# Two decode attention blocks on one core: the last projection of B transposed in its operands, and the first weight load cut in two

## The chip, the core and the metric

The kernel runs on one NeuronCore of a Trainium2 chip. The metric is the device time of one execution in microseconds (us), lower is better. Five engines work side by side, each with its own instruction queue: TensorE (PE; its weight loads are listed as PEld), VectorE (DVE), ScalarE (ACT), GpSimd (POOL) and SyncE (SP). Engines wait for each other through semaphores. Transfers between the chip's memory (HBM) and the core's on-chip memory (SBUF, 128 partitions) are issued by an engine, here SP and ACT, and carried out by 16 DMA engines. TensorE writes to PSUM, from where DVE or ACT copy results.

## What is computed

Two independent attention blocks, A and B, each for one query token with 32 heads of 128 elements, over a cache of 8192 positions. Their outputs, 512 numbers each, are put side by side.

```python
q = (x @ wq).reshape(B, Sq, H, Dh).transpose(0, 2, 1, 3)       # x: 1x1x512, wq: 512x4096
scores = einsum("bhqd,bhkd->bhqk", q, k_cache) * Dh ** -0.5    # k_cache: 1x32x8192x128, bf16
p = softmax(scores, axis=-1)
o = einsum("bhqk,bhkd->bhqd", p, v_cache)
y = o.transpose(0, 2, 1, 3).reshape(B, Sq, H * Dh) @ wo        # wo: 4096x512
out = concatenate([yA, yB], axis=-1)                           # 1x1x1024
```

The caches are 64 MiB each, four of them; each of the four weight matrices has 4 MiB. All of it is read once.

## The kernel before

The 64 heads are worked off in 16 rounds of 4 heads, n = 0 to 15; rounds 0 to 7 belong to A. Each round has an 8 MiB tile of k and one of v, both laid out so that a head's 8192 positions lie in 32 partitions with 256 positions each. There are two buffers for k and one for v.

**Start.** ACT issues the two loads of x (1 KB each, one row each), SP the two loads of wq (128 rows of 32 KB each, into the v buffer, which is still free), then k of rounds 0 and 1. TensorE spreads x over the partitions (`xmm`, L264), ACT copies it out (L268), and TensorE multiplies it with wq, 32 instructions for A and 32 for B (`qmm`, L281); in these a group of 4 heads writes 4 times 32 rows of PSUM, so that the query stands repeated in all partitions of its head. ACT copies the queries to SBUF (L287). The load of v of round 0 waits for the last of these matmuls, since it overwrites wq.

**A round.** DVE multiplies k with the query in place (L311, four pieces), TensorE adds up over the 128 elements with an identity matrix (L468), DVE finishes the sums (L316). The maximum goes over DVE and TensorE (L323, L488, L324, L327, L491), ACT takes exponentials (L339), TensorE adds up their sums (L497) and multiplies with v in 256 instructions (L505, 128 columns of weights and 4 moving columns). DVE divides (L345, L346) into `oD`, the attention output with the element within a head in the partitions and the head in the columns.

**SP's order** sets the order of the transfers: SP issues loads one behind another, and each waits for its buffer. k of round n + 2 waits for the sums of round n, v of round n for the v products of round n - 1. In the last rounds come wo of A, the first half of wo of B (group 0), v of round 15 in two pieces, then the rest of wo of B in five ever smaller groups (`WOB`: heads 16 to 23, 24 to 27, 28 and 29, 30, 31). wo of both blocks lies in the first k buffer.

**End.** The output of the earlier rounds is laid out anew for the groups whose rows were loaded as contiguous pieces (`relayout`, L390 to L396). In round 15 TensorE runs, between its scores and its v products, the projection of A (`mm_a`, L409: for each head one column of o repeated 32 times as weights and 512 columns of wo moving, four heads in turn into four blocks of 32 rows), the projection of B for group 0 (`mm_b`, L422) and the sum over the rows of A (L431). After the v products come groups 1 to 5 of `mm_b`. In `mm_b` a piece of wo (128 x 128) is the weight and one column of o moves past it; the result is a column of 128 outputs, four of them side by side in `yps[1]`, one per quarter of the outputs. Then DVE casts these four columns to `yT` (L441), TensorE transposes them to four rows (L442), DVE casts those into `out_b` (L444), and SP stores `out_b` (4 rows of 256 bytes). SP then waits for both stores.

A line number L208 stands for all DMA issues, since a helper records them; L53 is the wait in the emitter, and L534 the start of the engines' programs.

Of the kernel before, what the change touches and what calls it, by code (L numbers as in the profile page):

```python
# [8 lines left out]
BF16 = mybir.dt.bfloat16  # L9
F32 = mybir.dt.float32  # L10

P = 128
# [11 lines left out]
class _Plan:  # L24
# [6 lines left out]
    def wait(self, eng, mark):  # L31
        if mark is None:
            return
        ctr, val = mark
        if val <= 0 or self.waited.get((eng, ctr.name), 0) >= val:
            return
        self.waited[(eng, ctr.name)] = val
        self.prog[eng].append((None, ctr, val))

    def op(self, eng, fn, ctr=None, needs=(), inc=1):  # L40
        for m in needs:
            self.wait(eng, m)
        self.prog[eng].append((fn, ctr, inc))
        if ctr is None:
            return None
        ctr.n += inc
        return ctr, ctr.n
# [28 lines left out]
def bass_concat_heads__mha_block_cached__gqa_block_cached__decode_kernel(  # L76
# [13 lines left out]
    xs = [A_x, B_x]  # L90
    ks = [A_k_cache, B_k_cache]
    vs = [A_v_cache, B_v_cache]
    wqs = [A_wq, B_wq]
    wos = [A_wo, B_wo]
    NA = 2
    H, Sk, Dh = ks[0].shape[1:]
    D = xs[0].shape[2]
    NOUT = wos[0].shape[1]
# [5 lines left out]
    HP = P // G  # L104
# [3 lines left out]
    N = NA * GA  # L108
# [9 lines left out]
    NQ = NOUT // P  # L118

    with ExitStack() as st:  # L120
# [3 lines left out]
        def sb(name, shape, dt):  # L124
            return ec(nc.sbuf_tensor(name, shape, dt))
# [6 lines left out]
        wq_buf = [vflat[:, a * WQ:(a + 1) * WQ] for a in range(NA)]  # L132
        wq_sb = [b.rearrange("p (c n) -> p c n", c=C) for b in wq_buf]
        wo_buf = [kflat[0][:, a * H * NOUT:(a + 1) * H * NOUT] for a in range(NA)]
        wo_sb = [b.rearrange("p (j n) -> p j n", n=NOUT) for b in wo_buf]
# [6 lines left out]
        xrow = sb("xrow", [1, NA, D], BF16)  # L142
# [4 lines left out]
        ident = sb("ident", [P, P], BF16)  # L147
# [7 lines left out]
        oD = sb("oD", [P, NA, H], BF16)  # L155
        zb = sb("zb", [P, 2, P], BF16)
        o2 = sb("o2", [P, NA, H], BF16)
        mask = {g: sb("mask%d" % g, [P, P // g], BF16) for g in RG}
        jsel = {g: sb("jsel%d" % g, [P, g], BF16) for g in RG}
        yT = sb("yT", [P, NQ], BF16)  # L160
        out_a = sb("out_a", [1, NOUT], BF16)
        out_b = sb("out_b", [NQ, P], BF16)

        def ps(name, shape):
            return ec(nc.psum_tensor(name, shape, F32))
# [4 lines left out]
        bmp = ps("bmp", [P, 512])  # L170
        misc = ps("misc", [P, 512])
        yps = [ps("yps%d" % i, [P, 512]) for i in range(2)]

        pl = _Plan()
        op, wait = pl.op, pl.wait

        def ctr(name):
            return _Ctr(nc, st, name)

        s_x = ctr("s_x")  # L180
        s_w = [ctr("s_w%d" % a) for a in range(NA)]
# [4 lines left out]
        s_out = [ctr("s_out%d" % a) for a in range(NA)]  # L186
        c_pool, c_dve, c_act, c_pe = ctr("c_pool"), ctr("c_dve"), ctr("c_act"), ctr("c_pe")
# [19 lines left out]
        def dma(eng, dst, src, c, needs=()):  # L207
            return op(eng, lambda e: e.dma_start(dst, src), c, needs, inc=16)  # L208


        def const(fn, needs=()):
# [6 lines left out]
            out=ident[:], in_=ones_bf[:], pattern=[[1, P]], compare_op=ALU.is_equal,  # L218
            fill=0.0, base=0, channel_multiplier=-1), [i_onesb])
        i_identf = const(lambda e: e.affine_select(  # L220
            out=ident_f[:], in_=ones_f[:], pattern=[[1, P]], compare_op=ALU.is_equal,
# [2 lines left out]
        i_pool = const(lambda e: e.memset(pt[:], 0.0))  # L224


        x_in = [dma("ACT", xrow[0:1, a, :], xs[a][0], s_x) for a in range(NA)][-1]
        wq_in = [dma("SP", wq_buf[a], wqs[a].rearrange("(p c) n -> p (c n)", p=P), s_w[a])
                 for a in range(NA)]
        k_in, v_in = {}, {}  # L230

        def load_k(n):
# [34 lines left out]
        m = op("PE", xmm, c_pe, [x_in, i_pool])  # L267
# [39 lines left out]
        mul_done, sr_done, p_done, o_done = {}, {}, {}, {}  # L307
# [104 lines left out]
        m = op("PE", mm_a, c_pe, [o2_ready[0, 0], woa_in, y_free[0]])  # L412
        ya_ready = op("DVE", lambda e: e.tensor_copy(ya_sb, yps[0][:]), c_dve, [m, mul_done[N - 1, NB - 1]])

        def mm_b(g):
            h0, n, rows = WOB[g]

            def mm(e):
                r = None
                for j in range(h0, h0 + n):  # L420
                    for i in range(NQ):
                        r = e.matmul(yps[1][:, i:i + 1], wo_sb[1][:, j, i * P:(i + 1) * P],  # L422
                                     (o2 if rows else oD)[:, 1, j:j + 1], start=(j == 0 and i == 0),
                                     stop=(j == H - 1 and i == NQ - 1), skip_group_check=True)
                return r
            return op("PE", mm, c_pe, [o2_ready.get((1, h0)) if rows else o_done[N - 1],
                                       wob_in[g], y_free[1]])

        for g in range(NPRE):
            mm_b(g)  # L430
        m = op("PE", lambda e: e.matmul(mtp[0:1, :], part[:], ya_sb, start=True, stop=True),  # L431
               c_pe, [ya_ready, misc_free[0]])
        m = op("ACT", lambda e: e.copy(out_a[:], mtp[0:1, :]), c_act, [m])
# [4 lines left out]
        plan_o(N - 1)  # L438
        for g in range(NPRE, len(WOB)):
            m = mm_b(g)  # L440
        m = op("DVE", lambda e: e.tensor_copy(yT[:], yps[1][:, 0:NQ]), c_dve, [m])  # L441
        m = op("PE", lambda e: e.matmul(bmp[0:NQ, 0:P], yT[:], ident[:], start=True, stop=True),  # L442
               c_pe, [m, p_done[N - 1]])
        m = op("DVE", lambda e: e.tensor_copy(out_b[:], bmp[0:NQ, 0:P]), c_dve, [m])  # L444
        done_b = dma("SP", out[0][:, NOUT:2 * NOUT].rearrange("o (q n) -> (o q) n", q=NQ), out_b[:],
                     s_out[1], [m])
        wait("SP", done_a)
        wait("SP", done_b)

# [99 lines left out]
```

## Time and profile before

| what | value |
|---|---|
| median of 3 runs (lowest to highest) | 668.1 us (667.97 to 668.66) |
| the profiled execution's own time | 668.09 us |
| its span, first to last instruction | 666.4 us |
| mean granted TensorE clock | 0.71 |
| TensorE busy / its weight loads / VectorE / ScalarE | 61% / 36% / 52% / 9% |
| moved by DMA | 285.33 MB, mean 428 GB/s |

The profile is one execution recorded by the hardware profiler. Its time outside the span (668.09 - 666.4 = 1.7 us) holds no instruction. "PE" rows are matmuls, "PEld" rows weight loads; a row of the timeline gives the start, the length, the engine, the line, the operation with its output and inputs, how many instructions were merged, and in brackets how long the engine was idle before and what released it. SPq and ACTq rows are DMA issues. A row of the windows gives for a stretch the busy time and the number of instructions of each engine, the granted clock, the share of the 16 DMA engines that packets cover (all of a packet's length is put down to the stretch in which it starts, so short stretches can exceed 1) and the rate.

### The profile page before, as it was taken

How to read it: one execution, taken by the hardware profiler on the slowest of the kernel's cores; microseconds unless marked ns; L12 is line 12 of the kernel's file. 1: busy time of each engine (PE TensorE's matmuls, PEld its weight loads, DVE VectorE, ACT ScalarE, POOL GpSimd, SP SyncE). 2: the span in 40 equal slices, each digit the busy share in tenths (PEclk: the TensorE clock that was granted, in tenths of full speed). 3: DMA queues.
4: the chain of work that ended last, by engine and by line, in shares of the span. 5: the costliest groups of instructions: out<-in, count | busy, mean ns of one | idle time of the engine just before them, and what ended most of it. 6: DMA issues, size and time to landing. Idle time of an engine off the chain costs nothing.

```text
span 666.4 us, 11727 instructions
## 1 busy us (share of the span) xinstructions
PE 409.6 (61%) x5455; PEld 240.8 (36%) x5455; DVE 344.9 (52%) x230; ACT 62.4 (9%) x151; POOL 2.1 (0%) x11
## 2 busy tenths in 40 slices
PE   2217375774919377491937649292864929386788
PEld 1002152534316153431515343151524325152536
DVE  1046845648192744819274481918447291754730
ACT  1100202010020201002020100202020020202020
POOL 1000000000000000000000000000000000000000
PEclk9657768595867758586775859677595956759595
DMA  9999999999999999999999999999999999999996
GB/s 378 441 441 438 438 435 437 417 421 441 433 433 441 437 441 429 425 425 441 433 433 437 437 441 433 417 433 441 433 429 441 437 441 429 421 433 426 420 458 271
DMA packets 6342, 285.33 MB, mean 428 GB/s; under 512 B 699, under 2 KB 1214, under 8 KB 1342
## 3 DMA queue, kind: packets, MB, share of 16 engines
q1 hardware_dynamic: 6328, 285.22, 99.2%
q8 instruction: 5, 0.08, 0.0%
q14 instruction: 3, 0.02, 0.0%
q10 hardware_dynamic: 6, 0.00, 0.0%
HBM read 285.21 MB, written 0.00 MB: 428 GB/s over the span
## 4 chain that ended last, share of the span: by engine, by line
DMA 77%; PE 17%; DVE 3%; another core or an unknown queue 1%; issue 1%; ACT 1%; SPq 1%
DMA vn<-in_A_v_cache_dram 33%; DMA vn<-in_B_v_cache_dram 33%; PE acc L505 16%; DMA k<-in_A_k_cache_dram 6%; DMA k<-in_B_wo_dram 5%; DVE k L311 3%; PE rps L468 1%; ACT pt L339 1%; SPq L208 1%; DVE s_sb L316 0%; PE misc L497 0%; DVE m L323 0%; PE mtp L488 0%; PE bmp L491 0%
## 5 line engine op out<-in xcount | busy, mean ns | idle before, releaser
L311 DVE TENSOR_TENSOR k<-k,qmem 128x8192 bf16<-128x8192 bf16 x64 | 278.6, 4406 | 38.8 <-DMA k<-in_A_k_cache_dram 38.8
L468 PE MATMUL rps<-k,ident 128*128 128x512 bf16 x1024 | 259.2, 420 | 28.1 <-DVE k L311 20.2
L505 PE MATMUL acc<-pt,vn 128*128 128x4 bf16 x4096 | 111.9, 166 | 117.7 <-DMA vn<-in_A_v_cache_dram 61.6
L468 PEld LDWEIGHTS rps<-k,ident 128*128 128x128 bf16 x1024 | 107.5, 106 | 174.0 <-issue 51.6
L316 DVE TENSOR_REDUCE s_sb<-rps 128x64 f32<-128x512 f32 x64 | 44.2, 691 | 216.4 <-PE rps L468 216.4
L505 PEld LDWEIGHTS acc<-pt,vn 128*128 128x128 bf16 x4096 | 110.7, 104 | 119.0 <-DMA vn<-in_A_v_cache_dram 62.3
L332 ACT ACTIVATE negb<-bmp 128x1 f32<-128x1 f32 x16 | 2.7, 171 | 562.7 <-PE bmp L491 562.7
L339 ACT ACTIVATE pt<-s_sb,negb 32x256 bf16<-32x256 f32 x64 | 55.0, 859 | 1.9
L497 PE MATMUL misc<-rsum,ones_f 128*128 128x4 f32 x32 | 9.0, 351 | 58.7 <-ACT pt L339 58.7
L497 PEld LDWEIGHTS misc<-rsum,ones_f 128*128 128x128 f32 x32 | 8.0, 311 | 61.3 <-issue 61.3
L346 DVE TENSOR_TENSOR oD<-acc,rinv 128x4 bf16<-128x4 f32 x16 | 2.6, 162 | 44.7 <-PE acc L505 44.6
L488 PE MATMUL mtp<-ident_f,m 128*1 128x128 f32 x32 | 6.1, 271 | 19.8 <-DVE m L323 19.8
L339 ACT ACTIVATION_READ_ACCUMULATOR pt<-s_sb,negb 32x1 f32 x64 | 15.9, 249 | 0.0
L281 PE MATMUL yps<-vn,xb 128*32 128x512 bf16 x64 | 7.3, 630 | 10.5 <-DMA vn<-in_B_wq_dram 6.0
L491 PE MATMUL bmp<-ones_f,gmx 1*128 1x1 f32 x32 | 6.6, 272 | 9.9 <-DVE gmx L327 9.9
L488 PEld LDWEIGHTS mtp<-ident_f,m 128*1 128x1 f32 x32 | 1.4, 81 | 27.7 <-DVE m L323 27.7
L491 PEld LDWEIGHTS bmp<-ones_f,gmx 1*128 1x128 f32 x32 | 5.2, 203 | 14.6 <-DVE gmx L327 14.6
L324 DVE TENSOR_REDUCE gm<-mtp 1x4 f32<-1x128 f32 x16 | 4.5, 278 | 7.5 <-PE mtp L488 7.5
L281 PEld LDWEIGHTS yps<-vn,xb 128*32 128x32 bf16 x64 | 2.7, 134 | 14.2 <-issue 7.3
L323 DVE TENSOR_REDUCE m<-s_sb 128x1 f32<-128x256 f32 x16 | 6.7, 420 | 0.5
L264 PE MATMUL misc<-ones_bf,xrow 1*128 1x32 bf16 x8 | 0.4, 191 | 8.3 <-DMA xrow<-in_B_x_dram 8.3
L345 DVE RECIPROCAL rinv<-misc 128x4 f32<-128x4 f32 x16 | 2.6, 165 | 3.4 <-PE misc L497 3.4
(39 smaller groups left out, 31.5 us busy)
## 6 DMA issues: line engine op xcount, KB each, us to landing
vn<-in_B_v_cache_dram SPq DMA_DIRECT2D x2, 6144.0 KB, 26.9
vn<-in_A_wq_dram SPq DMA_DIRECT2D x1, 4096.0 KB, 12.3
vn<-in_B_wq_dram SPq DMA_DIRECT2D x1, 4096.0 KB, 21.6
vn<-in_B_v_cache_dram SPq DMA_DIRECT2D x2, 2048.0 KB, 31.4
k<-in_A_wo_dram SPq DMA_DIRECT2D x1, 4096.0 KB, 25.0
k<-in_B_wo_dram SPq DMA_DIRECT2D x1, 2048.0 KB, 29.5
k<-in_B_wo_dram SPq DMA_DIRECT2D x1, 1024.0 KB, 33.5
k<-in_B_wo_dram SPq DMA_DIRECT2D x1, 512.0 KB, 34.3
```

Of the source, the lines that this page charges most:

```text
L208: return op(eng, lambda e: e.dma_start(dst, src), c, needs, inc=16)
L281: r = e.matmul(yps[j % 2][hh * HP:(hh + 1) * HP, :].rearrange("p (i d) -> p i d", d=Dh), xb[:, a, c, :], w, start=(c == 0), stop=(c == C - 1))
L311: mul_done[n, h] = op("DVE", lambda e: e.tensor_tensor(k, k, qbc[:, n:n + 1, :].broadcast_to([P, HT, Dh]), ALU.mult), c_mul, [k_in[n], qbc ...
L316: sr_done[n, h] = op("DVE", lambda e: e.tensor_reduce(s_sb[:, h * HT:(h + 1) * HT], rps[:, h % 2, :].rearrange("p (t d) -> p t d", d=DW), ...
L323: op("DVE", lambda e: e.tensor_reduce(m1[:], s_sb[:], AX.X, ALU.max), c_g)
L324: m = op("DVE", lambda e: e.tensor_reduce(gm[:], mtp[0:1, 0:P].rearrange("o (h p) -> o h p", h=G), AX.X, ALU.max), c_dve, [gx_done(n)])
L339: p_done[n] = op("ACT", lambda e, h=h, q=q: e.activation(pt[q, :, h], s_sb[q, :], AF.Exp, bias=negb[q, n:n + 1], scale=scale, accum_out=rs ...
L468: r = e.matmul(rps[:, h % 2, :].rearrange("p (t d) -> p t d", d=DW), ident[:], kn[slot][:, h * HT:(h + 1) * HT, i * DW:(i + 1) * DW], star ...
L488: e.matmul(mtp[0:1, 0:P], m1[:], ident_f[:], start=True, stop=True).then_inc(c_gx.sem, 1)
L491: e.matmul(bmp[:, 0:1], gmx[:], ones_f[0:1, 0:1], start=True, stop=True).then_inc(c_bc.sem, 1)
L497: e.matmul(misc[:, 0:G], ones_f[:], rsum[:], start=True, stop=True).then_inc(c_sum.sem, 1)
L505: m = e.matmul(acc[:, 0:G], vn[:, t, :], pt[:, t, :], start=(t == 0), stop=(t == T - 1))
```

## The change

`mm_b` swaps its operands: a column of o, repeated 32 times by a step of zero, is the weight, and 128 columns of wo move. Quarter i of the outputs goes to rows 32 i to 32 i + 31 of `yps[1]`, all 32 rows of a quarter being equal. The transposition with `yT` falls away: DVE casts all 128 rows into `out_b`, and the store takes rows 0, 32, 64 and 96. At the start the load of wq of A becomes two, of 16 and of 112 rows, on the same semaphore, and the two loads of x move from ACT's queue to SP's, behind both pieces of wq of A and ahead of wq of B.

```diff
-        yT = sb("yT", [P, NQ], BF16)
-        out_b = sb("out_b", [NQ, P], BF16)
+        out_b = sb("out_b", [P, P], BF16)
...
-        x_in = [dma("ACT", xrow[0:1, a, :], xs[a][0], s_x) for a in range(NA)][-1]
-        wq_in = [dma("SP", wq_buf[a], wqs[a].rearrange("(p c) n -> p (c n)", p=P), s_w[a])
-                 for a in range(NA)]
+        wq_in = []
+        for a in range(NA):
+            src = wqs[a].rearrange("(p c) n -> p (c n)", p=P)
+            for p0, p1 in ((0, 16), (16, P)) if a == 0 else ((0, P),):
+                m = dma("SP", wq_buf[a][p0:p1, :], src[p0:p1, :], s_w[a])
+            wq_in.append(m)
+            if a == 0:
+                x_in = [dma("SP", xrow[0:1, i, :], xs[i][0], s_x) for i in range(NA)][-1]
...
-                        r = e.matmul(yps[1][:, i:i + 1], wo_sb[1][:, j, i * P:(i + 1) * P],
-                                     (o2 if rows else oD)[:, 1, j:j + 1], start=(j == 0 and i == 0),
-                                     stop=(j == H - 1 and i == NQ - 1), skip_group_check=True)
+                        r = e.matmul(yps[1][i * HP:(i + 1) * HP, 0:P],
+                                     (o2 if rows else oD)[:, 1, j:j + 1].broadcast_to([P, HP]),
+                                     wo_sb[1][:, j, i * P:(i + 1) * P],
+                                     start=(j == 0), stop=(j == H - 1))
...
-        m = op("DVE", lambda e: e.tensor_copy(yT[:], yps[1][:, 0:NQ]), c_dve, [m])
-        m = op("PE", lambda e: e.matmul(bmp[0:NQ, 0:P], yT[:], ident[:], start=True, stop=True),
-               c_pe, [m, p_done[N - 1]])
-        m = op("DVE", lambda e: e.tensor_copy(out_b[:], bmp[0:NQ, 0:P]), c_dve, [m])
-        done_b = dma("SP", out[0][:, NOUT:2 * NOUT].rearrange("o (q n) -> (o q) n", q=NQ), out_b[:],
-                     s_out[1], [m])
+        m = op("DVE", lambda e: e.tensor_copy(out_b[:], yps[1][:, 0:P]), c_dve, [m])
+        done_b = dma("SP", out[0][:, NOUT:2 * NOUT].rearrange("o (q n) -> (o q) n", q=NQ),
+                     out_b[0:P:HP, :], s_out[1], [m])
```

## Prediction

> **What bounds the kernel now.** I read the page first, for which resource is full from end to end.
>
> ```profile
> span 666.4 us, 11727 instructions
> DMA  9999999999999999999999999999999999999996
> q1 hardware_dynamic: 6328, 285.22, 99.2%
> q8 instruction: 5, 0.08, 0.0%
> ```
>
> The 16 DMA engines are busy in every slice but the last; queue q1, SP's loads, covers 99.2% of the span. No engine comes near this. So the end is the start of the stream, plus the bytes at a steady rate, plus what follows the last byte. The change leaves the bytes as they are (one load becomes two of the same rows), so only its two ends can move. The chain of waits, cut to its last stretch, shows the second end:
>
> ```profile
> 629.38 34.18 DMA k<-in_B_wo_dram
> ...
> 663.61 0.28 PE yps L422 x4
> 663.91 0.17 DVE yT L441
> 664.13 0.28 PE bmp L442
> 664.43 0.28 DVE out_b L444
> ```
>
> The last piece of wo of B lands at 663.56. Four matmuls, a cast, a transposition and a cast follow; the store is issued at 664.74 (row below), and the span ends 1.66 us later. The first end is in the timeline of the first microseconds:
>
> ```profile
> 0.80 0.51 ACTq L208 DMA_DIRECT2D xrow<-in_A_x_dram  x1
> 0.80 0.40 SPq L208 DMA_DIRECT2D vn<-in_A_wq_dram  x1
> 1.26 0.41 SPq L208 DMA_DIRECT2D vn<-in_B_wq_dram  x1
> 1.35 0.22 ACTq L208 DMA_DIRECT2D xrow<-in_B_x_dram  x1
> ...
> 8.32 0.44 PE L264 MATMUL misc<-ones_bf,xrow 1*128 1x32 bf16 x8 [8.32 <-DMA xrow<-in_B_x_dram]
> 8.80 0.37 ACT L268 CAST xb<-misc 128x256 bf16<-128x256 f32 x1 [5.93 <-PE misc L264]
> ...
> 13.26 3.64 PE L281 MATMUL yps<-vn,xb 128*32 128x512 bf16 x32 [4.49 <-DMA vn<-in_A_wq_dram]
> ...
> 22.88 3.64 PE L281 MATMUL yps<-vn,xb 128*32 128x512 bf16 x32 [5.98 <-DMA vn<-in_B_wq_dram]
> ...
> 26.61 0.33 SPq L208 DMA_DIRECT2D vn<-in_A_v_cache_dram  x1
> ```
>
> Two equal weight matrices arrive 22.88 - 13.26 = 9.62 us apart, which is the steady price of 4 MiB. The first needed 13.26 - 0.80 = 12.46 us from its issue, so 2.84 us go to getting started and to landing. Where they go, the windows show:
>
> ```profile
> core 0: us, PE busy (x) PEld busy (x) DVE busy (x) ACT busy (x) POOL busy (x), PEclk, DMA share, GB/s
> 1.60:1.80 0.20, 0.00 (x0) 0.00 (x0) 0.20 (x2) 0.20 (x1) 0.20 (x3) 1.00 0.02 5
> 1.80:2.20 0.40, 0.00 (x0) 0.00 (x0) 0.40 (x4) 0.40 (x1) 0.40 (x1) 1.00 4.72 1229
> ...
> 2.60:2.80 0.20, 0.00 (x0) 0.00 (x0) 0.20 (x2) 0.20 (x1) 0.07 (x1) 1.00 0.44 164
> ...
> 3.60:4.30 0.70, 0.00 (x0) 0.00 (x0) 0.00 (x0) 0.00 (x0) 0.00 (x0) 1.00 1.73 749
> ...
> 4.80:5.50 0.70, 0.00 (x0) 0.00 (x0) 0.00 (x0) 0.00 (x0) 0.00 (x0) 1.00 1.73 749
> ```
>
> A packet counts where it starts. 1229 GB/s times 0.40 us is 492 KB, fifteen packets of 32 KB (one row of wq each); 164 times 0.20 is the sixteenth. So each DMA engine starts its first row between 1.8 and 2.8. The sixteen second rows start at 3.6 to 4.3, the third at 4.8 to 5.5: the first row took about 1.9 us, later ones 1.2. The 1 KB of x of A stands at 1.6 to 1.8.
>
> **The change, start.** Removed: two ACT issues (0.51 and 0.22 us). Added on SP, past which x moves: the issue of the 112 rows (some 0.40 us, as its two wq neighbours), then x twice (0.22 to 0.51 each). wq of B and k of rounds 0 and 1 are issued 0.8 to 1.4 us later, but wq of B is needed on the wire only near 12 us: covered. Without that cover it would cost those 1.4 us.
>
> x now lands behind 4 MiB, near 12.7 to 13.3 instead of 8.32. The wait is TensorE's first; behind it stand the x matmuls (0.44), ACT's copy (0.37) and all of L281. The products of A then begin near 13.26 + 0.9 = 14.2 and end near 17.8, ahead of wq of B at 22.88, so the last product, and with it the issue of v at 26.61, stays. Cost: nothing, hidden by 22.88 - 17.8 = 5 us of waiting for wq of B. The two x rows add 2 KB to one DMA engine, nothing beside its share of 285.22 / 16 = 17.8 MB.
>
> What the small first load gains isn't in the trace. Bound from above: the first row could be as quick as later ones (1.9 - 1.2 = 0.7), and it could start as early as the 1 KB of x, 0.1 to 0.3 before the rows of wq: together -1.0 us. Bound from below: rows 16 and up are issued 0.4 later and start some 0.6 to 1.5 behind the end of their issue at 1.6, that is 2.2 to 3.1, while the first rows end at 3.0 at the earliest: at most +0.1. I take -0.3: the head start that the x row shows, and a little of the long first row, since 16 cold first rows stay 16 cold first rows.
>
> [...]
>
> **The change, end.** Removed from the chain: cast L441, transposition L442 and their gaps, from 663.91 to 664.43: -0.52 us. L444 stays, with as many elements a partition (128), now over 128 partitions: 0.28 as before. The store still has 4 rows. The work before it:
>
> ```profile
> 648.73 1.83 PE L409 MATMUL yps<-k,o 128*32 128x512 bf16 x16
> ...
> 650.50 1.86 PE L422 MATMUL yps<-o,k 128*128 128x1 bf16 x64
> ...
> 654.53 6.97 PE L505 MATMUL acc<-pt,vn 128*128 128x4 bf16 x256
> ...
> 661.36 1.49 PE L422 MATMUL yps<-o,k 128*128 128x1 bf16 x48
> ...
> 663.04 0.84 PE L422 MATMUL yps<-oD,k 128*128 128x1 bf16 x16 [0.18 <-DMA k<-in_B_wo_dram]
> ...
> 664.74 0.35 SPq L208 DMA_DIRECT2D out_dram<-out_b  x1
> ...
> L409 PEld LDWEIGHTS yps<-k,o x32: 92/97/150, 647.9 to 649.5; 128*32 128x32 bf16 x32
> L422 PEld LDWEIGHTS yps<-o,k x112: 103/104/115, 650.5 to 662.7; 128*128 128x128 bf16 x112
> L281 PE MATMUL yps<-vn,xb x64: 586/634/634, 13.3 to 25.9; 128*32 128x512 bf16 x64
> L442 PE MATMUL bmp<-ident,yT x1: 267/267/267, 664.1 to 664.1; 128*4 128x128 bf16 x1
> ```
>
> From 650.50 TensorE runs almost without a pause to about 662.85, and its next group lands at about 663.0: nearly no slack. So the pace of the new 32-row matmuls counts twice, in the 64 of group 0 and in the 64 behind the v products. Call g the time of four of them, one per quarter. The nearest rows are L281 and L409, which also fill four blocks of 32 rows, with 512 columns: 32 in 3.64 us, the last 0.634 long, gives (3.64 - 0.634) / 7 = 0.43 us for four. 128 columns are a quarter: g = 0.107. The old form takes 1.49 / 12 = 0.124 for four, the last drain in it. Bounds: weight loads of 0.097 to 0.150 us that don't hide behind such short matmuls give g = 0.107 + 0.150 = 0.257; if the four quarters don't overlap, g = 0.43.
>
> Group 0 then takes 16 g for 1.86, and 16 more g stand behind the v products. The last group of four ends at 661.36 + (16 g - 1.86) + 16 g + 0.16 (0.267 of L442 less a pace), or, if wo lands later than that, at 663.61 + 0.27 + 0.02 = 663.90, against 663.89 before. Both meet at 32 g = 4.24, g = 0.13. Below it the end saves its whole 0.52; at g = 0.149 nothing; at 0.257 it costs 661.36 - 1.86 + 8.22 + 0.16 - 663.89 - 0.52 = +3.5 us. I take g = 0.107, because L409 and L281 show weight loads of the same 32 columns hidden, and the end's term as -0.5.
>
> [...] L409's 32-column loads of 0.097 us are no slower than the 0.104 of 128 columns in this trace (mean of L422), so the loads as such cost the same; only their hiding is open, and that is the third rival below.
>
> **Sum.** 668.09 - 0.3 - 0.5 = 667.3 us. The profiled execution equals the median of the runs (668.1), so no shift between them. That is 0.12% below; 0.2% (1.3 us) is about what a measurement of this kernel can tell from no change.
>
> **Rivals.** (1) The start gains its whole bound: 668.09 - 1.0 - 0.5 = 666.6. For it: 2.84 us between issue and pace are a lot, and the first rows are 0.7 longer than later ones. Against: one row per engine has still to start. (2) Nothing arrives: the split gains 0, and g near 0.15 gives the 0.52 back, 668.1. For it: TensorE has no slack after 650.50. (3) Slower: TensorE becomes the bound of the end. It decides from g = 0.19 (32 g = 4.24 + 0.52 + 1.3); at g = 0.257 the time is 668.09 - 0.3 + 3.5 = 671.3. For it: no row has 128 columns in 32-row blocks, with a weight load for each 0.107 us of streaming; against: L409 hides four loads in each 0.43 us. (4) The stream's own skew. All engines carry equal bytes, yet they don't end together:
>
> ```profile
> 661.50:662.00 0.50, 0.50 (x25) 0.50 (x22) 0.16 (x1) 0.00 (x0) 0.00 (x0) 0.50 0.41 145
> ...
> 662.50:663.00 0.50, 0.35 (x14) 0.27 (x11) 0.00 (x0) 0.00 (x0) 0.00 (x0) 0.50 0.17 59
> ```
>
> From 661.5 to 663 only some are still at work: 1.5 us of skew or more, which foreign packets such as the five of the instruction queue may leave on a few engines. If a changed program puts two of them on one engine or none, the end moves by up to that either way; near its whole, 1.3 us, gives 668.6 or 666.0.
>
> **How the numbers follow.** Forecast 0.55, with its own range 666.8 to 667.8; rival 1 0.18; rival 2 0.13; rival 3 0.08; rival 4 0.06, half each way. Faster by over 0.2% (below 666.8): rival 1, half of 4 and 0.05 of the forecast, 0.26. Slower by over 0.2% (above 669.4): rival 3 and a little of 2 and 4 on top of the sum's noise, 0.12. Within: 0.62. The range 666.3 to 669.0 holds the forecast, rivals 1 and 2 and half of 4; it leaves out rival 3.
>
> **What would show it.** Start: the first packets at 1.6 to 2.0 and wq of A's products at about 14.2, with wq of B still ready at 22.6 or so, at most 0.3 earlier; if it is 22.88, the split gained nothing, if 21.9, rival 1. End: groups of four at 0.107 us in the v-side stretch, the last wo landing followed by 0.3 of TensorE and 0.28 of DVE, and the store issued 0.7 us after the landing instead of 1.18. A last matmul more than 0.5 us behind the landing of wo is rival 3. A landing of wo moved by over 1 us with an unmoved wq of B is rival 4 and would make the prediction wrong.

## The result and the profile after

The changed kernel takes 676.92 us (median of 4 runs, 676.71 to 677.23) against 668.19 before: a ratio of 1.013, 95% interval 1.0113 to 1.0148. It is slower by 8.7 us, where 667.3 was forecast. The profiled execution took 676.71 us with a span of 675.0.

The changed kernel's line numbers are its own: L207 stands for the DMA issues, L285 for `qmm`, L427 for `mm_b`, L447 for the cast into `out_b`. The timeline of the first microseconds shows the loss at once:

```profile
0.81 0.86 SPq L207 DMA_DIRECT2D vn<-in_A_wq_dram  x2
1.71 0.33 SPq L207 DMA_DIRECT2D xrow<-in_A_x_dram  x1
2.35 0.36 SPq L207 DMA_DIRECT2D vn<-in_B_wq_dram  x1
...
21.82 0.44 PE L268 MATMUL misc<-ones_bf,xrow 1*128 1x32 bf16 x8 [21.82 <-DMA xrow<-in_B_x_dram]
22.73 3.64 PE L285 MATMUL yps<-vn,xb 128*32 128x512 bf16 x32 [0.46 <-ACT xb L272]
...
31.97 3.64 PE L285 MATMUL yps<-vn,xb 128*32 128x512 bf16 x32 [5.61 <-DMA vn<-in_B_wq_dram]
```

x, behind wq of A, lands at 21.8 us, not at 13. wq of B is there at 31.97, not at 22.88: the stream is 9.09 us late before the first round has begun. The issues themselves are early enough. The windows (the columns are those of the prediction) show a slow stream from the first row on, first the kernel before, then the changed one:

```profile
5.50:8.00 2.50, 0.00 (x0) 0.00 (x0) 0.00 (x0) 0.00 (x0) 0.00 (x0) 1.00 0.97 420
8.00:12.00 4.00, 0.44 (x8) 0.34 (x8) 0.00 (x0) 0.37 (x1) 0.00 (x0) 1.00 0.91 393
12.00:16.00 4.00, 2.74 (x28) 1.43 (x32) 0.00 (x0) 0.59 (x1) 0.00 (x0) 1.00 0.99 426
16.00:20.00 4.00, 0.90 (x11) 0.00 (x0) 0.00 (x0) 0.59 (x1) 0.00 (x0) 1.00 1.12 483
```

```profile
1.80:2.20 0.40, 0.00 (x0) 0.00 (x0) 0.40 (x3) 0.28 (x1) 0.40 (x1) 1.00 9.16 1311
...
2.80:4.30 1.50, 0.00 (x0) 0.00 (x0) 0.65 (x6) 0.00 (x0) 0.00 (x0) 1.00 0.00 0
4.30:5.50 1.20, 0.00 (x0) 0.00 (x0) 0.00 (x0) 0.00 (x0) 0.00 (x0) 1.00 1.07 191
5.50:8.00 2.50, 0.00 (x0) 0.00 (x0) 0.00 (x0) 0.00 (x0) 0.00 (x0) 1.00 0.60 118
8.00:12.00 4.00, 0.00 (x0) 0.00 (x0) 0.00 (x0) 0.00 (x0) 0.00 (x0) 1.00 1.02 262
12.00:16.00 4.00, 0.00 (x0) 0.00 (x0) 0.00 (x0) 0.00 (x0) 0.00 (x0) 1.00 1.11 303
16.00:20.00 4.00, 0.00 (x0) 0.00 (x0) 0.00 (x0) 0.00 (x0) 0.00 (x0) 1.00 0.92 221
```

From 5.5 to 20 us the share of the DMA engines averages 0.94 while the rate is 118 to 303 GB/s instead of some 430. So the engines aren't waiting for work: each packet takes longer. All sixteen first rows start at 1.8 to 2.2 (1311 GB/s times 0.40 us is 524 KB, sixteen rows of 32 KB), but no second row starts before 4.3.

The last stretch of the changed kernel's chain of waits (start, length, what), and then its timeline:

```profile
672.22 0.33 PE yps L427 x4
...
672.57 0.29 DVE out_b L447
```

```profile
658.98 1.11 PE L427 MATMUL yps<-k,o 128*32 128x128 bf16 x64
...
669.67 1.05 PE L427 MATMUL yps<-k,o 128*32 128x128 bf16 x32 [0.60 <-DMA k<-in_B_wo_dram]
...
672.22 0.11 PEld L427 LDWEIGHTS yps<-k,oD 128*32 128x32 bf16 x4 [0.21 <-DMA k<-in_B_wo_dram]
672.57 0.29 DVE L447 CAST out_b<-yps 128x128 bf16<-128x128 f32 x1 [3.30 <-PE yps L427]
672.89 0.61 SPq L207 DMA_DIRECT2D out_dram<-out_b  x1
```

The last piece of wo is used at 672.22 and the store is issued 0.67 us later; before it was 663.61 and 664.74, 1.13 us. That is 0.46 us of the forecast 0.5. But SP's issue now takes 0.61 us instead of 0.35, and from its start to the end of the span it is 675.0 - 672.89 = 2.11 us instead of 666.4 - 664.74 = 1.66. The 0.45 us are given back. From the last piece to the end of the span nothing has changed: 2.78 us against 2.79.

Of the 9.09 us of delay at 31.97, 8.61 are left at the last piece (672.22 - 663.61). Where in between the other 0.5 us were made up is open.

### The profile page after: what moved, and what is told of

Same layout as the page of the kernel before. It is cut to its first block, busy times and chain, and to the rows that moved or that the text cites. A ratio compares the mean times of both kernels' runs of the same rounds, so it can differ in the third digit from the quotient of the medians.

```text
span 675.0 us, 11724 instructions
## 1 busy us (share of the span) xinstructions
PE 409.6 (61%) x5454; PEld 239.3 (35%) x5454; DVE 344.8 (51%) x229; ACT 62.4 (9%) x151; POOL 2.1 (0%) x11
## 4 chain that ended last, share of the span: by engine, by line
DMA 77%; PE 17%; DVE 3%; issue 1%; another core or an unknown queue 1%; ACT 1%; SPq 0%
DMA vn<-in_A_v_cache_dram 32%; DMA vn<-in_B_v_cache_dram 32%; PE acc L508 16%; DMA k<-in_A_k_cache_dram 7%; DMA k<-in_B_wo_dram 5%; DVE k L315 3%; PE rps L471 1%; ACT pt L343 1%; SPq L207 0%; PE yps L427 0%; DVE s_sb L320 0%; PE misc L500 0%; DVE m L327 0%; PE mtp L491 0%
## 5 line engine op out<-in xcount | busy, mean ns | idle before, releaser
L268 PE MATMUL misc<-ones_bf,xrow 1*128 1x32 bf16 x8 | 0.4, 191 | 21.8 <-DMA xrow<-in_B_x_dram 21.8
L285 PE MATMUL yps<-vn,xb 128*32 128x512 bf16 x64 | 7.3, 630 | 6.1 <-DMA vn<-in_B_wq_dram 5.6
L494 PEld LDWEIGHTS bmp<-ones_f,gmx 1*128 1x128 f32 x32 | 4.8, 186 | 14.6 <-DVE gmx L331 14.6
L268 PEld LDWEIGHTS misc<-ones_bf,xrow 1*128 1x128 bf16 x8 | 0.3, 113 | 21.8 <-DMA xrow<-in_B_x_dram 21.8
L285 PEld LDWEIGHTS yps<-vn,xb 128*32 128x32 bf16 x64 | 2.6, 134 | 10.0 <-DMA vn<-in_B_wq_dram 6.5
```

The costliest lines, as they stand in the source:

```text
L285: r = e.matmul(yps[j % 2][hh * HP:(hh + 1) * HP, :].rearrange("p (i d) -> p i d", d=Dh), xb[:, a, c, :], w, start=(c == 0), stop=(c == C - 1))
L494: e.matmul(bmp[:, 0:1], gmx[:], ones_f[0:1, 0:1], start=True, stop=True).then_inc(c_bc.sem, 1)
```

## The experiments

The theory after the result: how fast a transfer goes depends on which partitions it writes. Rivals: the reading side (a stretch of HBM too narrow, or an odd share of 7 rows an engine), x on SP's queue, and two loads instead of one as such. The runs on the start keep the end as before.

**The two ends apart.** The start as before, the end as changed (the edit against the changed kernel):

```diff
-        wq_in = []
...
-                x_in = [dma("SP", xrow[0:1, i, :], xs[i][0], s_x) for i in range(NA)][-1]
+        x_in = [dma("ACT", xrow[0:1, a, :], xs[a][0], s_x) for a in range(NA)][-1]
+        wq_in = [dma("SP", wq_buf[a], wqs[a].rearrange("(p c) n -> p (c n)", p=P), s_w[a])
+                 for a in range(NA)]
```

> The start is as before, the end as changed. If the loss sits in the start alone: 668.2 us plus what the end gives, and the landing of wq of B back at 22.9 us. For the end the changed kernel's trace shows the store issued 0.72 us after the last landing (1.18 before), but 2.1 us from the issue to the end of the span (1.66 before): so 667.9 to 668.5, no change. Rival: the new matmuls cost TensorE time at the end, then more than 669.

668.12 us, ratio 0.9997 (0.9988 to 1.0006). The median shows neither a cost nor a gain from the end. Its timeline ends like that of the changed kernel:

```profile
653.61 6.82 PE L503 MATMUL acc<-pt,vn 128*128 128x4 bf16 x256 [1.26 <-DMA vn<-in_B_v_cache_dram]
...
660.99 1.04 PE L422 MATMUL yps<-k,o 128*32 128x128 bf16 x32 [0.56 <-DMA k<-in_B_wo_dram]
...
663.95 0.29 DVE L442 CAST out_b<-yps 128x128 bf16<-128x128 f32 x1 [3.32 <-PE yps L422]
664.26 0.63 SPq L207 DMA_DIRECT2D out_dram<-out_b  x1
```

TensorE now waits for v (1.26 us) and for wo (0.56). How much of this slack the new matmuls gave can't be told from the two profiles, since TensorE was granted a clock of 1.00 here from 650.0 to 651.1 and of 0.50 in the kernel before from 650.5 to 652.3; with the old end (e3_x below), at 0.84 from 650.5 to 652.2, it waited for wo as well, 0.45 us.

**The cut alone**, x on ACT as before (from here on the edits are against the kernel before, unless said otherwise):

```diff
...
+            for p0, p1 in ((0, 16), (16, P)) if a == 0 else ((0, P),):
+                m = dma("SP", wq_buf[a][p0:p1, :], src[p0:p1, :], s_w[a])
...
```

> Only wq of A in two loads of 16 and 112 rows; x stays on ACT's queue, the end as before. If the cut by rows is the cause (on whichever side of the transfer): the first rows take 3 to 4 us instead of 1.9, the rows of the second load about 2.1 us instead of 1.2, wq of B is there at about 32 us, total 676.8 to 677.3. If x behind the weights is the cause: 668.2 and wq of B at 22.9.

676.65 us, ratio 1.0126 (1.0107 to 1.0144): the whole loss.

**x alone** on SP, behind an uncut wq of A:

```diff
-        x_in = [dma("ACT", xrow[0:1, a, :], xs[a][0], s_x) for a in range(NA)][-1]
...
+            wq_in.append(dma("SP", wq_buf[a], src, s_w[a]))
+            if a == 0:
+                x_in = [dma("SP", xrow[0:1, i, :], xs[i][0], s_x) for i in range(NA)][-1]
```

> Only x moved to SP's queue behind an uncut wq of A. If the cut is the cause: 668.2 within 0.3, x at about 13 us, the products of A from about 14, wq of B at 22.9. If x is the cause: wq of B at about 32 and 677.

668.08 us, ratio 0.9999 (0.9990 to 1.0009). x lands at 13.1 and costs nothing, as the prediction had it for its part.

**The same sizes, cut by columns**, x following on SP:

```diff
...
+            for n0, n1 in ((0, WQ // 8), (WQ // 8, WQ)) if a == 0 else ((0, WQ),):
+                m = dma("SP", wq_buf[a][:, n0:n1], src[:, n0:n1], s_w[a])
...
```

> wq of A in two loads of the same sizes (1/8 and 7/8), but cut by columns, so that each load goes to all 128 partitions; x follows on SP, the end as before. If what hurts is that a load reaches a part of the partitions: 667.9 to 668.3, wq of B at 22.6 to 23.2. If it is having two loads on one semaphore, or the smaller descriptors of a cut load: wq of B near 32 and 677.

668.06 us, ratio 1.0000 (0.9990 to 1.0009). Two loads as such cost nothing; wq of B is there at 22.66, 0.2 earlier than before. The profiled execution, one of the two slowest with 668.74 us, ends 0.6 us later all the same, by another path: its chain holds no transfer from 619.6 on, and from 648.35 it runs through TensorE alone up to the last matmul:

```profile
648.35 3.54 PE yps L414 x32
651.89 1.80 PE yps L427 x64
653.69 1.80 PE mtp L436 x2
655.48 0.52 PE misc L502 x2
656.00 6.83 PE acc L510 x256
662.83 1.72 PE yps L427 x64
```

That is the missing slack of the old end, seen as a bound, at a granted clock of 0.50 from 648.3 to 653.7. Times like this one are not rare: of the 104 executions with the old end and a start that isn't slowed (the kernel before, e3_x, e4_cols and e5_dst128) 19 took more than 668.5 us, up to 669.16. Of the 43 with the new end and such a start (e1_tail, e10_store_act, e11_cols_tail and e13_one_row) none did; the longest took 668.38. So with the new end the long executions are gone, though the median stays; which part of it does this was not tried.

**Reading or writing.** The two loads read the same bytes as in the cut by rows, but write all 128 partitions, so that the rows of wq of A stand in the wrong places and A's output is wrong:

```diff
...
+                for r0, r1 in ((0, 64), (64, D)):
+                    n0, n1 = r0 * H * Dh // P, r1 * H * Dh // P
+                    m = dma("SP", wq_buf[a][:, n0:n1],
+                            wqs[a][r0:r1, :].rearrange("d (e n) -> (d e) n", n=128).rearrange(
+                                "(p f) n -> p (f n)", p=P), s_w[a])
...
```

> [...] If the writing side is what is slow (few partitions a load): wq of B at 22.5 to 23.2, total 667.9 to 668.5. If the reading side is slow (a narrow or oddly spaced stretch of HBM): wq of B near 32, total 676.7.

667.93 us, ratio 0.9998 (0.9987 to 1.0010), wq of B at 22.45. The same bytes of HBM are read in the same two loads, and now they are fast; which engine reads which stretch the trace doesn't show. The counterpart reads every eighth row into partitions 0 to 15, so that rows 0 to 15 of the weights and A's output are wrong:

```diff
...
+                dma("SP", wq_buf[a][0:16, :], src[0:P:8, :], s_w[a])
+                m = dma("SP", wq_buf[a][16:P, :], src[16:P, :], s_w[a])
...
```

> [...] If the writing side is slow: the first rows still take 3 to 4 us, total 676.5 to 677. If the reading side is slow: the first rows take 1.9 us as before, and the total falls by about 1.5 to 2 us, to 675.

676.51 us in its one execution. The time from issue to landing of the two loads is the last number of these rows of the DMA issues, first with 128 partitions written (e5_dst128), then with the reading spread (e7_src16):

```profile
vn<-in_A_wq_dram SPq DMA_DIRECT2D x1, 3584.0 KB, 11.4
vn<-in_A_wq_dram SPq DMA_DIRECT2D x1, 512.0 KB, 3.2
```

```profile
vn<-in_A_wq_dram SPq DMA_DIRECT2D x1, 3584.0 KB, 21.0
vn<-in_A_wq_dram SPq DMA_DIRECT2D x1, 512.0 KB, 7.0
```

The cut alone had 21.2 and 6.7: reading farther apart changes next to nothing, writing to all partitions does. So it is the writing side.

**How many partitions, or which.** Rows 0 to 63, then 64 to 127:

```diff
...
+            for p0, p1 in ((0, 64), (64, P)) if a == 0 else ((0, P),):
...
```

> wq of A cut into rows 0 to 63 and 64 to 127, x on ACT, the end as before. [...] If it is the narrow reading of the 16 rows or the odd share of 7 rows an engine: each half reads 2 MB in rows of 32 KB at the full rate, wq of B at 22.9 and 668.2.

678.45 us, ratio 1.0153 (1.0109 to 1.0197), wq of B at 33.32: far from the 668.2 expected of the reading side or the odd share. The next run has five loads: partitions 0, 4, ... 60; 64 to 127; then the three other classes of the lower half.

```diff
...
+            for p in ([slice(0, 64, 4), slice(64, P)] + [slice(i, 64, 4) for i in (1, 2, 3)]
+                      if a == 0 else [slice(0, P)]):
+                m = dma("SP", wq_buf[a][p, :], src[p, :], s_w[a])
...
```

> All rows of wq of A to their own partitions, in five loads: partitions 0, 4, ... 60; then 64 to 127; then 1, 5, ...; 2, 6, ...; 3, 7, ... [...] If it is only how few partitions a load has: 16 rows take 3 to 4 us in each of the four small loads, total near 683.

678.24 us in its one execution, where a mere count of partitions calls for 683. Its first 16 rows, four times as spread out, are done sooner than rows 0 to 15 of the changed kernel. In the stretch from 4.30 to 5.50, where that one started 7 second rows (191 GB/s times 1.20 us), this run started 14:

```profile
4.30:5.50 1.20, 0.00 (x0) 0.00 (x0) 0.00 (x0) 0.00 (x0) 0.00 (x0) 1.00 1.77 382
```

In all it is no better than the halves (678.45). Then 64 rows of another choice, 32 to 95, and the rest in two loads of 32 rows:

```diff
...
+            for p0, p1 in ((32, 96), (0, 32), (96, P)) if a == 0 else ((0, P),):
...
```

> wq of A in three loads: rows 32 to 95, then 0 to 31, then 96 to 127; x on ACT, the end as before. [...] If any load of 64 partitions is slow, as rows 0 to 63 were: the first load lands at 13 to 14 us, wq of B at 32.5 and 678.

673.53 us, ratio 1.0080 (1.0061 to 1.0098), far from the 678 expected if any load of 64 partitions is slow. The windows of the halves, then of this run:

```profile
2.80:4.30 1.50, 0.00 (x0) 0.00 (x0) 0.65 (x6) 0.08 (x1) 0.00 (x0) 1.00 0.99 219
4.30:5.50 1.20, 0.00 (x0) 0.00 (x0) 0.00 (x0) 0.00 (x0) 0.00 (x0) 1.00 1.19 246
5.50:8.00 2.50, 0.22 (x6) 0.22 (x7) 0.00 (x0) 0.00 (x0) 0.00 (x0) 1.00 1.02 210
8.00:12.00 4.00, 0.23 (x7) 0.12 (x4) 0.00 (x0) 0.37 (x1) 0.00 (x0) 1.00 0.94 197
```

```profile
2.80:4.30 1.50, 0.00 (x0) 0.00 (x0) 0.64 (x6) 0.08 (x1) 0.00 (x0) 1.00 0.88 372
4.30:5.50 1.20, 0.00 (x0) 0.00 (x0) 0.00 (x0) 0.00 (x0) 0.00 (x0) 1.00 1.02 437
5.50:8.00 2.50, 0.44 (x8) 0.34 (x8) 0.00 (x0) 0.37 (x1) 0.00 (x0) 1.00 1.32 419
8.00:12.00 4.00, 0.00 (x0) 0.00 (x0) 0.00 (x0) 0.00 (x0) 0.00 (x0) 1.00 0.71 147
12.00:16.00 4.00, 0.00 (x0) 0.00 (x0) 0.00 (x0) 0.00 (x0) 0.00 (x0) 1.00 1.16 246
```

Rows 0 to 63 go at 197 to 246 GB/s all the way; rows 32 to 95, just as many, at 372 to 437 until 8 us, and the two loads of 32 rows behind them fall to 147 to 246. The count isn't what decides; what makes rows 32 to 95 faster than rows 0 to 63, no run shows.

**The end.** The store from rows 0 to 3, and the strided store from ACT, each against the kernel with only the end changed:

```diff
-                     out_b[0:P:HP, :], s_out[1], [m])
+                     out_b[0:NQ, :], s_out[1], [m])
```

```diff
-        done_b = dma("SP", out[0][:, NOUT:2 * NOUT].rearrange("o (q n) -> (o q) n", q=NQ),
+        done_b = dma("ACT", out[0][:, NOUT:2 * NOUT].rearrange("o (q n) -> (o q) n", q=NQ),
```

> As e1_tail, but the store of B takes rows 0 to 3 of out_b instead of rows 0, 32, 64 and 96, so that all of B's output is its first quarter. If the step of 32 partitions makes SP's issue slow: issue 0.35 us instead of 0.63, the store's end 0.45 earlier, span 665.8. If not: 0.6 us and 666.3 again.

> As e1_tail, but ACT issues the store of B. If the slow issue belongs to SP, which has just been through its long list of issues: 0.25 us and an end 0.4 earlier, 667.7. If it belongs to the access with a step of 32 partitions: 0.5 to 0.6 us again, 668.1.

With rows 0 to 3 (the timeline of e9_store_rows below) the issue takes 0.35 us and the span is 665.8; the single run took 667.55 us:

```profile
663.53 0.11 PEld L422 LDWEIGHTS yps<-k,oD 128*32 128x32 bf16 x4 [0.21 <-DMA k<-in_B_wo_dram]
663.88 0.29 DVE L442 CAST out_b<-yps 128x128 bf16<-128x128 f32 x1 [3.33 <-PE yps L422]
664.20 0.35 SPq L207 DMA_DIRECT2D out_dram<-out_b  x1
```

From the last piece to the end it is now 2.27 us (665.8 - 663.53), against 2.79 before: the 0.5 us of the forecast. From ACT with the step of 32 partitions the issue takes 0.59 us and the time is 668.18 (ratio 0.9999, 0.9990 to 1.0009). The slow issue goes with the step, not with the engine.

**Both parts without their faults.** First the changed kernel with the cut by columns:

> The changed kernel with one difference: wq of A is cut by columns into 1/8 and 7/8 instead of by rows, so both loads go to all 128 partitions. If the loss was the partitions a load reaches: 676.9 falls to 667.6 to 668.0, wq of B at 22.5 to 22.9. If the new end and the new start together have a cost of their own: more than 668.5.

668.10 us, ratio 0.9999 (0.9990 to 1.0008), 0.1 above the upper figure expected for the kernel without the loss and below the 668.5 of the rival; wq of B is used at 22.8, and the store has its 0.61 us of issue. Then this with the quarters copied into one row:

```diff
...
-        m = op("DVE", lambda e: e.tensor_copy(out_b[:], yps[1][:, 0:P]), c_dve, [m])
...
+        ms = [op(("DVE", "ACT")[i % 2],
+                 lambda e, i=i: (e.tensor_copy if i % 2 == 0 else e.copy)(
+                     out_b[0:1, i * P:(i + 1) * P], yps[1][i * HP:i * HP + 1, 0:P]),
+                 (c_dve, c_act)[i % 2], [m]) for i in range(NQ)]
+        done_b = dma("SP", out[0][:, NOUT:2 * NOUT], out_b[:], s_out[1], ms[-2:])
```

> The changed kernel with wq of A cut by columns, and the end without the step of 32 partitions: DVE and ACT copy two quarters each into one row, and SP stores one row of 1 KB. If the step alone took back the 0.5 us of the new end: issue 0.3 to 0.35 us, 1.66 us from the issue to the end, two copies in a row cost 0.15 to 0.25 more than one: span 666.0 to 666.2, 667.6 to 667.9, which may not be told from before. If the end has another cost: issue or landing longer, 668.1 or more.

The timeline of its end:

```profile
663.58 0.11 PEld L427 LDWEIGHTS yps<-k,oD 128*32 128x32 bf16 x4 [0.21 <-DMA k<-in_B_wo_dram]
663.93 0.54 ACT L448 CAST out_b<-yps 1x128 bf16<-1x128 f32 x2 [11.02 <-PE yps L427]
663.93 0.60 DVE L448 CAST out_b<-yps 1x128 bf16<-1x128 f32 x2 [3.30 <-PE yps L427]
664.56 0.26 SPq L207 DMA_DIRECT2D out_dram<-out_b  x1
```

The issue is short (0.26 us), the copies cost 0.3 us more than one; the end is 2.5 us behind the last piece (666.1 - 663.58). 667.86 us, ratio 0.9995 (0.9986 to 1.0004): the lowest median of the complete versions beside a kernel before at 668.14, but not told from it.

## Why the prediction was wrong

The sum put the start at -0.3 us and the end at -0.5; the runs show some +9 for the start and nothing for the end's median. The view that the stream's two ends are all that can move held; nearly the whole loss stands at its first end, as 9.09 us by wq of B.

The step that failed is the lower bound of the start, "at most +0.1". It let the first rows end "at 3.0 at the earliest" and the rows behind them keep the 1.2 us a row of a load over all 128 partitions; that the pace depends on which partitions are written was not considered, and no rival had it. The runs put in its place: 512 KB into partitions 0 to 15 land 6.8 us after their issue (6.7 in the cut alone) where 128 partitions take 3.2; the 3584 KB of the second load land 21.0 us after theirs instead of 11.4.

One thing stays open, and it is the larger part. The second load lands 14.6 us behind the first (21.0 and 6.8 us from their issues, which are 0.4 us apart), where 112 rows dealt evenly to 16 engines, seven each, would take some 8.4 by an estimate from the 1.2 us a row of the kernel before. While it runs, at 221 to 303 GB/s in the windows, sixteen rows take 1.7 to 2.4 us. So about 6 of the 9.09 us belong to the 112 rows. In e5_dst128 the same bytes, written as 128 rows of 28 KB, land 8.6 us behind the first load (11.4 and 3.2), so the rows written make the difference; whether by where they lie or by their number, no run separates. How the rows are dealt out to the engines can't be seen in the views of the trace and was not tried; that all engines carry equal bytes, from which rival 4 started, is the author's estimate too.

x: it landed behind wq of A as said and cost nothing, under the cover that was named, the wait for wq of B. In e3_x the numbers are those of the prediction (x at 13.1, products at 14.0). In the changed kernel the products of A end at 22.73 + 3.64 = 26.4, and the later wq of B still covers them.

The end: g, the time of four matmuls, was taken as 0.107 us, the largest risk in the text. The 32 behind the v products give (1.05 - 0.314) / 7 = 0.105 at a granted clock of 0.50, with the longest matmul's 314 ns from this row of the changed kernel:

```profile
L427 PE MATMUL yps<-k,o x112: 219/220/314, 659.0 to 671.2; 128*32 128x128 bf16 x112
L427 PEld LDWEIGHTS yps<-k,o x112: 97/98/150, 658.6 to 671.1; 128*32 128x32 bf16 x112
```

So the weight loads, four of 0.097 us or more in each 0.105, hide, and rival 3 is out. The saving of 0.5 us up to the store came as forecast; what failed is the half sentence "The store still has 4 rows". Its rows lie 32 partitions apart, and that costs the 0.45 to 0.5 us again. Rival 2 had the end's saving come to nothing by a slow g; it did come to nothing, but by the store.

The gain of the split was taken as -0.3 us for the start. With all 128 partitions written wq of B is used at 22.79 (e11_cols_tail), 22.66 (e4_cols), 22.53 (e13_one_row) and 22.45 (e5_dst128), 0.1 to 0.4 us earlier than before; but uncut loads scatter too, from 22.75 (e9_store_rows) to 22.92 (e3_x). So about the forecast size may be there for a load that this kernel doesn't make; the medians don't show it.

## What to carry to other kernels

Where the transfers bound a kernel, look at which partitions each load writes before counting loads or bytes: rows 0 to 63 and 64 to 127 in turn took about twice the time of the whole here (wq of B at 33.32 us instead of 22.88), while a cut by columns cost nothing (22.66). And when a step at the end of the chain is taken away, read the operands of the step behind it too: the same four rows of 256 bytes needed some 0.45 us more from their issue to the end of the span when they lay 32 partitions apart, 0.26 of it in the issue.

## What had not been expected

- 64 partitions can be slow or fast: rows 0 to 63 ran at 197 to 246 GB/s and rows 32 to 95 at 372 to 437, with the same number of rows and bytes.
- The issue of a 1 KB store took 0.61 to 0.63 us on SP and 0.59 on ACT with a step of 32 partitions, 0.29 to 0.35 on SP with neighbouring rows and 0.26 from one row.
- Group 0's 64 matmuls with 128 columns, each with its own weight load, took 1.11 us in the changed kernel, 17 ns each, at a granted clock of 0.96. They follow the clock: 1.38 us at 0.77 (e9_store_rows) and 1.58 at 0.66 (e10_store_act). The old ones with one column hardly do: 1.86 us at 0.50 in the kernel before and 1.79 at 0.84 (e3_x).
